# z2's last gelu product and sums by VectorE, its squares by ScalarE; weights split ahead beside the V tiles; distances between loads

## The chip, the cores and the metric

The kernel runs on one core of a Trainium2 chip. The metric is the device time of one execution in microseconds (us), lower is better. A core has TensorE (PE in the profile; its weight loads are PEld), VectorE (DVE), ScalarE (ACT), GpSimd (POOL) and SyncE (SP), which here only issues DMA transfers, in order. Each engine runs its own instructions in the order in which the program lists them, and waits by semaphores for the others.

## The reference

Two branches work on the layer norm of the same x (2048 x 512) and are added to x: attention with 32 heads of 16 columns, and a gated mlp that mixes over the sequence.

```python
def _A_ref(x, wqkv, wo):
    q, k, v = ...                                   # 32 heads, Dh = 16
    scores = jnp.einsum("bhqd,bhkd->bhqk", q, k) * (Dh ** -0.5)
    p = _softmax(scores, axis=-1)
    o = jnp.einsum("bhqk,bhkd->bhqd", p, v)
    return o.transpose(0, 2, 1, 3).reshape(B, S, D) @ wo

def _B_ref(x, w_in, w_sp, b_sp, w_out):             # Fh = 896
    z = _gelu(jnp.einsum("bsd,df->bsf", x, w_in))
    z1 = z[..., :Fh]
    z2 = _layernorm(z[..., Fh:], axis=-1)
    g = jnp.einsum("ts,bsf->btf", w_sp, z2) + b_sp[None, :, None]
    return jnp.einsum("bsf,fd->bsd", z1 * g, w_out)

xn = _layernorm(x, axis=-1)
return x + _A_ref(xn, A_wqkv, A_wo) + _B_ref(xn, B_w_in, B_w_sp, B_b_sp, B_w_out)
```

The gelu is the one with tanh: z (1 + tanh(c (z + 0.044715 z^3))) / 2. The kernel leaves out the half, which the layer norm behind z2 takes out again (so its epsilon is 4 EPS).

## The kernel before

All products with float32 inputs are made of split operands: a high part and the rest (`hi`, `lo`), three products each, so a weight is loaded, copied by POOL (L291) and subtracted by POOL (L293) before TensorE can use it. Weights that are used later than they are split are stored to a DRAM copy and fetched again (`ahead_of_time`, `fetch_parts`: w1 to `w1scr`, the first eight blocks of the spatial weights to `wsscr`).

Attention handles the 32 heads as 16 pairs, each in 64 steps of scores, 1024 steps in all. A step is one score product (L1157), the exponential by ScalarE, and a share of the product with the values (L1258). Ahead of each group of scores runs the row maximum of the next: a product of its own (L1171) whose result VectorE reduces (`mm`, L872); the maxima `ms` go through DRAM (`mscr`) into a row of the queries (`qst`). All this is laid out in 128 **blocks**. A block holds 8 score items, 9 or 7 maxima items in turn, 24 **dense** slots, and at its end a run of 32 matmuls with the values. `ORDER` holds the two patterns, as strings of S, M, D and V.

The dense slots are filled from a queue of generators: `v_rest`, `qk_rest` (queries and keys of the later heads), `z2_all` (16 tiles of 128 rows, 896 columns), `z1_all`, `spatial` (4 groups of 512 rows, 7 units each), `mlp_out`, `attn_out`. Where the queue has nothing ready, the planner writes a **filler** (L1230), two matmuls with a zero weight that add nothing; they keep TensorE busy.

The order of all engines is fixed when the program is built, by a planner. It counts the time of TensorE in `T["P"]` and gives each piece of other work to an engine's clock (`yield "A", us` for ScalarE, `"D"` VectorE, `"G"` POOL) or to a condition (`"C"`); the microseconds there are its own assumptions. Work of low rank on ScalarE and VectorE is placed only in the time of a values run, unless it is older than `AGE` (`may`). The conditions test the planner's time (`clock`) and free buffers (`room`, changed by `lease`): `room["big"]` counts the free buffers of one SBUF ring, from which weights, z tiles and temporaries come. None of this runs on the chip: what runs is the order, with semaphores for data that one engine hands to another and for buffers.

A z2 tile (`z2_norm`, L511) goes from ScalarE (square) to POOL (L518, L520), to ScalarE (tanh), to POOL (L524: 1 + tanh; L526: times z), to VectorE (two `bn_stats` L533, one `bn_aggr` L535), to POOL (six operations of one column, L539 to L544, then the normalised tile as high part and rest, L550 to L554 for 512 and for 384 columns), and by SP to DRAM (`z2scr`), from where the spatial products fetch it as `zs`.

Of the kernel before, what the change touches and what calls it, by code (L numbers as in the profile page):

```python
# [16 lines left out]
P = 128  # L17
# [19 lines left out]
LATE = 24  # L37
LEAD = 30
# [5 lines left out]
AGE = 6.0  # L44
# [16 lines left out]
def fused_block(ctx, tc, x, wqkv, wo, w_in, w_spT, b_sp, w_out, out):  # L61
# [219 lines left out]

    def weight(out, k, a, spare):
        yield "C", lambda: raws[0] < DEEP and room["big"] > 1 + spare[0]
# [23 lines left out]
    def fetch_parts(out, k, scr, spare):  # L307
        yield "C", lambda: room["big"] > 1 + spare[0]
        t = piece(f"wf{len(out)}_{len(wsp)}")
        move(t, scr)  # L310
        yield "T", LOAD
        out[k] = t
# [134 lines left out]
    def qk_rest():  # L447
        for f in range(NF):
            owed[0] += 1
            spawn(ahead_of_time(f, (f"w1_{f}", w_in[:, f * P:(f + 1) * P], D, ND), w1scr[f], AHEAD), 1)  # L450
        for g in (2, 3, 0, 1):
            for m in range(1, 4):
                if m == 2 and g in (3, 0):
                    fetch_xnT((g + 1) % NG, 0.5)
# [4 lines left out]
                if (g, m) in ((3, 1), (0, 1)):  # L459
                    for s in range(KEPT // 2) if g else range(KEPT // 2, KEPT):  # L460
                        owed[0] += 1
                        spawn(ahead_of_time(s, sp_weights(0, s), wsscr[s], AHEAD), 1)
# [26 lines left out]
    def v_rest():  # L489
        for t in range(EARLY, NT, 2):  # L490
# [4 lines left out]
            if t in (2, 6):  # L495
                lease("big", 4)
            yield "e", [v_out(t + b, b) for b in range(2)]
# [13 lines left out]
    def z2_norm(t, z):  # L511
# [5 lines left out]
        yield "G", 1.0  # L517
        nc.gpsimd.tensor_scalar(u, u, 0.044715, 1.0, ALU.mult, ALU.add)  # L518
        yield "G", 2.1
# [3 lines left out]
        yield "G", 1.2  # L523
        nc.gpsimd.tensor_scalar(u, u, 1.0, 1.0, ALU.add, ALU.mult)  # L524
        yield "G", 2.1
        nc.gpsimd.tensor_mul(z, u, z)  # L526
        lease("big", 1)
        st = sm.tile([P, 2, 6], F32, tag="zst", name=f"zst{t}", bufs=6)
        mv = sm.tile([P, 2], F32, tag="zmv", name=f"zmv{t}", bufs=6)
        rs = sm.tile([P, 3], F32, tag="zrs", name=f"zrs{t}", bufs=6)  # L530
        for j in range(2):
            yield "D", 0.62
            nc.vector.bn_stats(st[:, j, :], z[:, j * 448:(j + 1) * 448])  # L533
        yield "D", 0.1
        nc.vector.bn_aggr(mv, st)  # L535
        yield "G", 1.6
        g = nc.gpsimd
        v, r, q, m = rs[:, 0:1], rs[:, 1:2], rs[:, 2:3], mv[:, 0:1]
        g.tensor_scalar(v, mv[:, 1:2], 1.0, 4 * EPS, ALU.mult, ALU.add)  # L539
# [4 lines left out]
        g.tensor_scalar(q, m, r, -1.0, ALU.mult, ALU.mult)  # L544
        for j, (lo, w) in enumerate(((0, 512), (512, 384))):
# [3 lines left out]
            yield "G", 0.0012 * w  # L549
# [828 lines left out]
```

## Time and profile before

| | |
|---|---|
| median of 3 runs | 1856.94 us (1855.68 to 1857.37) |
| profiled execution, its own time | 1855.84 us |
| its span (first to last instruction) | 1853.9 us |
| first values run of attention begins | 114.77 us |
| last values run of 32 matmuls begins | 1805.56 us |
| granted TensorE clock | 0.999 |

The span is what the profile divides into shares. "Busy" is the time in which an engine ran an instruction. The prediction reads three more kinds of rows. In the chain of waits, a row is the start, the length, and what ran or was waited for, followed back from the last instruction of the kernel; `x32` counts matmuls of one line in a row, and `SPq` is a DMA issue on SP's queue. In a group of instructions, `out<-in` names the tiles, then come the shape, the count, the total time, the mean in ns, and the idle time of the engine before them with what ended it. In the timeline, a bracket at the end of a row is the idle time before that instruction and what ended it.

Each group of spatial products uses its own 16 blocks of weights. Around a change of group the blocks 61, 75 and 89 hold 19, 19 and 16 dense slots, and the two or three after each of them up to 27; block 22 in the z2 stage holds none.

### The profile page before, as it was taken

To read this page: it belongs to the slowest core of one execution; us is meant where nothing else is said; L and a number is where in the kernel's file an instruction comes from. 1 tells how busy PE (TensorE), PEld (TensorE's weight loads), DVE (VectorE), ACT (ScalarE), POOL (GpSimd) and SP (SyncE) were. 2 spreads that over 40 slices of the span, in tenths; PEclk is the share of its full clock that TensorE was granted. 3 is DMA by queue.
4 is the path that set the end of the run, shared out by engine and by line. 5 is a ranking of instruction groups with operands and counts; after the bars stand their busy time and mean duration, and the time that the engine had idled before them with its cause. 6 is when DMAs were issued, how large, how long until landed. Compare 5 with 4: busy or idle time off the path is not lost.

```text
span 1853.9 us, 38030 instructions
## 1 busy us (share of the span) xinstructions
PE 1807.5 (97%) x14778; PEld 1093.5 (59%) x14778; DVE 1440.9 (78%) x1677; ACT 1189.6 (64%) x1292; POOL 722.0 (39%) x808
## 2 busy tenths in 40 slices
PE   6999999999999999999999999999999999999998
PEld 4766566655655565556556665666656556565543
DVE  6578778888888787877878787787778878787883
ACT  2157777687776777666666665666656666565665
POOL 5324342778888777222452135102522240002200
PEclk9999999999999999999999999999999999999999
DMA  7728872533565246656867558565767667575422
GB/s 236 288 93 283 277 238 87 127 91 112 133 217 137 100 119 201 152 160 154 219 171 199 156 180 217 155 146 154 194 164 186 177 173 148 149 175 143 130 86 80
DMA packets 212124, 306.14 MB, mean 165 GB/s; under 512 B 36816, under 2 KB 108048, under 8 KB 209056
## 3 DMA queue, kind: packets, MB, share of 16 engines
q1 hardware_dynamic: 202824, 273.83, 53.8%
q0 software_dynamic: 9120, 29.89, 4.7%
q8 instruction: 116, 1.90, 0.4%
q14 instruction: 64, 0.52, 0.1%
HBM read 193.80 MB, written 109.85 MB: 164 GB/s over the span
## 4 chain that ended last, share of the span: by engine, by line
PE 87%; DVE 5%; DMA 2%; ACT 2%; issue 1%; POOL 1%; SPq 1%; DVEq 0%; ACTq 0%; POOLq 0%
PE dps L1216 35%; PE sl L1258 23%; PE sl L1157 14%; PE sl L1171 12%; DVE mm L872 3%; SPq L134 1%; PE dps L1230 1%; ACT pf L78 1%; DMA zs<-z2scr 1%; POOL wsp L293 0%; DMA wsp_11r<-in_w_spT 0%; PE sl L247 0%; PE sl L246 0%; PE sl L245 0%; PE sl L1016 0%
## 5 line engine op out<-in xcount | busy, mean ns | idle before, releaser
L872 DVE TENSOR_REDUCE mm<-sl 128x2 f32<-128x1024 f32 x1024 | 1223.8, 1222 | 202.2 <-PE sl L1171 195.8
L78 ACT ACTIVATE pf<-sl 128x1024 f32<-128x1024 f32 x1024 | 1041.6, 1026 | 335.1 <-PE sl L1157 298.5
L1258 PE MATMUL sl<-pf,vall 128*32 128x512 f32 x4096 | 467.9, 595 | 1.0 <-DVE on L1006 0.6
L1157 PE MATMUL sl<-qst,kst 50*128 50x512 f32 x2048 | 436.0, 418 | 9.4 <-DVE mm L872 2.9
L1171 PE MATMUL sl<-kst,qst 48*128 48x512 f32 x2048 | 422.1, 405 | 4.5 <-DVE mm L872 2.4
L1216 PE MATMUL dps<-wsp,zs 64*128 64x512 f32 x2352 | 379.0, 392 | 1.6 <-DMA zs<-z2scr 1.5
L1157 PEld LDWEIGHTS sl<-qst,kst 50*128 50x128 f32 x2048 | 194.3, 184 | 221.9 <-issue 79.6
L1258 PEld LDWEIGHTS sl<-pf,vall 128*32 128x32 f32 x4096 | 119.3, 109 | 266.9 <-issue 234.3
L1171 PEld LDWEIGHTS sl<-kst,qst 48*128 48x128 f32 x2048 | 195.1, 185 | 105.0 <-ACT pf L78 52.6
L1216 PEld LDWEIGHTS dps<-wsp,zs 64*128 64x128 f32 x2352 | 226.9, 187 | 39.3 <-DMA zs<-z2scr 2.2
L78 ACT ACTIVATE e<-sl 128x512 f32<-128x512 f32 x64 | 38.3, 598 | 205.2 <-PE sl L1258 198.0
L1280 DVE TENSOR_TENSOR e<-sl,e 128x512 f32<-128x512 f32 x64 | 44.3, 692 | 134.3 <-PE sl L1258 76.3
L778 POOL TENSOR_TENSOR hhl<-z1i,hhl 128x512 fp32r<-128x512 f32 x28 | 36.1, 1297 | 267.1 <-ACT hhl L78 267.0
L1216 PE MATMUL dps<-w,xt 64*128 64x448 f32 x768 | 110.4, 368 | 1.5
L1216 PE MATMUL dps<-wout,hp 64*128 64x512 f32 x672 | 110.5, 393 | 0.0
L923 POOL TENSOR_TENSOR ob<-ob 128x512 f32<-128x512 f32 (+1 forms) x16 | 20.6, 1285 | 195.2 <-DMA ob<-rscr 195.2
L1216 PEld LDWEIGHTS dps<-w,xt 64*128 64x128 f32 x768 | 73.5, 186 | 16.3 <-issue 7.8
L1216 PEld LDWEIGHTS dps<-wout,hp 64*128 64x128 f32 x672 | 65.8, 187 | 9.2
L919 POOL TENSOR_TENSOR ob<-ob 128x512 f32<-128x512 f32 (+1 forms) x16 | 20.6, 1287 | 101.6 <-DMA ob<-escr 100.9
L443 POOL TENSOR_TENSOR qkhl<-qr,qkhl 128x512 fp32r<-128x512 f32 x24 | 30.3, 1282 | 70.4 <-ACT qkhl L78 66.3
L1216 PE MATMUL dps<-wf,zs 64*128 64x512 f32 x336 | 55.5, 393 | 0.1
L1216 PE MATMUL dps<-xnT,wqk 64*128 64x512 f32 x288 | 47.7, 396 | 1.1 <-ACT vall L78 0.4
(289 smaller groups left out, 1688.3 us busy)
## 6 DMA issues: line engine op xcount, KB each, us to landing
zs<-z2scr SPq DMA_DIRECT2D x192, 256.0 KB
escr<-e SPq DMA_DIRECT2D x60, 256.0 KB
hscr<-hhl POOLq DMA_DIRECT2D x28, 512.0 KB, 6.4
qst<-qscr SPq DMA_DIRECT2D x30, 384.0 KB
kst<-kscr SPq DMA_DIRECT2D x30, 384.0 KB
qscr<-qkhl SPq DMA_DIRECT2D x16, 512.0 KB
kscr<-qkhl SPq DMA_DIRECT2D x16, 512.0 KB
xscr<-xnT POOLq DMA_DIRECT2D x16, 512.0 KB, 4.8
```

The costliest lines, as they stand in the source:

```text
L78: return nc.scalar.activation(out, in_, func, **kw)
L134: nc.sync.dma_start(raw(dst), raw(src))
L443: nc.gpsimd.tensor_sub(hl[:, 1, :], raw_, hl[:, 0, :].bitcast(F32))
L778: nc.gpsimd.tensor_sub(hl[:, 1, :], z1, hl[:, 0, :].bitcast(F32))
L872: nc.vector.tensor_reduce(mmax[g][:, :, t, kc], sl[k], AX.X, ALU.max)
L919: nc.gpsimd.tensor_add(both_[rows, 0, :], both_[rows, 0, :], both_[rows, 1, :])
L923: nc.gpsimd.tensor_mul(both_[rows, 0, :], both_[rows, 0, :], both_[rows, 1, :])
L1157: nc.tensor.matmul(sl[k][:, j, :], kst[p % 2][rows, kt * P:(kt + 1) * P], qst[p % 2][rows, c * 512:(c + 1) * 512], start=True, stop=True)
L1171: nc.tensor.matmul(sl[k][:, j, :], qst[p % 2][rows, tt * P:(tt + 1) * P], kst[p % 2][rows, kc * 512:(kc + 1) * 512], start=True, stop=True)
L1216: nc.tensor.matmul(dps[:, bank, :w], lhs, rhs, start=go, stop=stop)
L1258: nc.tensor.matmul(sl[k][cols:cols + VW, 0, :], vpack(kt + r, 2 * p + j), pf[:, j * 512:(j + 1) * 512], start=n % CYC == 0, stop=n % CYC = ...
L1280: nc.vector.tensor_add(e, sl[k][:, 0, :], e)
```

## The change

Three things are changed, and the planner's assumed costs with them.

1. **z2.** VectorE forms (tanh + 1) z in two halves of 448 columns, and the same instruction gives the sum of each half. POOL adds the two sums to a negative mean (one column). ScalarE squares z minus the mean over 896 columns, and the same instruction gives the sum of squares. The two wide POOL operations (L524, L526) and the `bn_stats` and `bn_aggr` are gone, and `u` is handed back one step later.
2. **Splitting ahead.** The loads, splits and stores of w1 (seven) and of the first eight spatial weight blocks are asked for behind V tile 6 (`VAHEAD`) in place of inside `qk_rest`.
3. **Distances.** `bulk(us)` notes that the road is taken for so long in the planner's time, `clear()` asks whether it is free: weights keep 1 us, fetched parts and z loads 2 us. A z load that is needed next goes at once. `AGE` goes from 6 to 9, and one fetch of xnT from 0.5 to 1.5.

```diff
--- before.py
+++ after.py
@@ -35,13 +35,14 @@
 DEEP = 4
 ZROOM = 4
 LATE = 24
+VAHEAD = 6
 LEAD = 30
 KEPT = 8
 OUTS = 8
 XAT = 8.0
 XBY = 2.0
 AHEAD = (1,)
-AGE = 6.0
+AGE = 9.0
 GATED = "AD"
 ORDER = ('SMDDSDDMDSDDMDDSDMDDSDMDDSDMDDSDMDDSDDMDMV', 'SMDDDDSDMDDSDMDDSDMDDSDMDDDSDMDDSDDDDMSV')
 PF = 8
@@ -279,8 +280,17 @@
     raws = [0]
     owed = [0]
 
+    road = [0.0]
+
+    def clear():
+        return clock() >= road[0]
+
+    def bulk(us):
+        road[0] = max(road[0], clock()) + us
+
     def weight(out, k, a, spare):
-        yield "C", lambda: raws[0] < DEEP and room["big"] > 1 + spare[0]
+        yield "C", lambda: clear() and raws[0] < DEEP and room["big"] > 1 + spare[0]
+        bulk(1.0)
         raws[0] += 1
         rw = begin(*a)
         n = rw.shape[1]
@@ -305,7 +315,8 @@
         after(2.5, lease, "big", 1)
 
     def fetch_parts(out, k, scr, spare):
-        yield "C", lambda: room["big"] > 1 + spare[0]
+        yield "C", lambda: clear() and room["big"] > 1 + spare[0]
+        bulk(2.0)
         t = piece(f"wf{len(out)}_{len(wsp)}")
         move(t, scr)
         yield "T", LOAD
@@ -445,21 +456,14 @@
         after(2.5, lease, "hilo", 1)
 
     def qk_rest():
-        for f in range(NF):
-            owed[0] += 1
-            spawn(ahead_of_time(f, (f"w1_{f}", w_in[:, f * P:(f + 1) * P], D, ND), w1scr[f], AHEAD), 1)
         for g in (2, 3, 0, 1):
             for m in range(1, 4):
                 if m == 2 and g in (3, 0):
-                    fetch_xnT((g + 1) % NG, 0.5)
+                    fetch_xnT((g + 1) % NG, 1.5)
                 if m == 3 and g == 1:
                     z2_load(0)
                     z2_load(1)
                 yield from need(lambda: (m, 1) in wq)
-                if (g, m) in ((3, 1), (0, 1)):
-                    for s in range(KEPT // 2) if g else range(KEPT // 2, KEPT):
-                        owed[0] += 1
-                        spawn(ahead_of_time(s, sp_weights(0, s), wsscr[s], AHEAD), 1)
                 if g == 1 and m == 1:
                     prepare(w2, [((c, j), f"w2_{c}_{j}", w_in[c * P:(c + 1) * P, FH + j * 448: FH + (j + 1) * 448], 448) for c in range(ND) for j in range(2)], spare=(2,))
                 ops = [lambda c, w=wq[m, a]: (w[:, 0, c * P:(c + 1) * P], w[:, 1, c * P:(c + 1) * P], xnT[g, c][:, 0, :], xnT[g, c][:, 1, :]) for a in range(2)]
@@ -494,6 +498,13 @@
             yield from both(ND, ops(t), ops(t + 1))
             if t in (2, 6):
                 lease("big", 4)
+            if t == VAHEAD:
+                for f in range(NF):
+                    owed[0] += 1
+                    spawn(ahead_of_time(f, (f"w1_{f}", w_in[:, f * P:(f + 1) * P], D, ND), w1scr[f], AHEAD), 1)
+                for s in range(KEPT):
+                    owed[0] += 1
+                    spawn(ahead_of_time(s, sp_weights(0, s), wsscr[s], AHEAD), 1)
             yield "e", [v_out(t + b, b) for b in range(2)]
             yield "q",
 
@@ -514,43 +525,42 @@
         u = piece(f"z2u{t}").bitcast(F32).rearrange("p a b -> p (a b)")[:, :FH]
         yield "A", ta(FH)
         act(u, z, AF.Square)
-        yield "G", 1.0
+        yield "G", 0.98
         nc.gpsimd.tensor_scalar(u, u, 0.044715, 1.0, ALU.mult, ALU.add)
-        yield "G", 2.1
+        yield "G", 2.2
         nc.gpsimd.tensor_mul(u, u, z)
         yield "A", ta(FH)
         act(u, u, AF.Tanh, scale=GC)
-        yield "G", 1.2
-        nc.gpsimd.tensor_scalar(u, u, 1.0, 1.0, ALU.add, ALU.mult)
-        yield "G", 2.1
-        nc.gpsimd.tensor_mul(z, u, z)
+        st = sm.tile([P, 5], F32, tag="zst", name=f"zst{t}", bufs=6)
+        rs = sm.tile([P, 3], F32, tag="zrs", name=f"zrs{t}", bufs=6)
+        g = nc.gpsimd
+        a, b, m, square, v = (st[:, i:i + 1] for i in range(5))
+        for j, half in enumerate((a, b)):
+            cols = slice(j * 448, (j + 1) * 448)
+            yield "D", 0.63
+            nc.vector.scalar_tensor_tensor(z[:, cols], u[:, cols], 1.0, z[:, cols], ALU.add, ALU.mult, accum_out=half)
+        yield "G", 0.6
+        g.tensor_scalar(m, a, b, -1.0 / FH, ALU.add, ALU.mult)
+        yield "A", ta(FH) + 0.2
+        act(u, z, AF.Square, bias=m, accum_out=square)
         lease("big", 1)
-        st = sm.tile([P, 2, 6], F32, tag="zst", name=f"zst{t}", bufs=6)
-        mv = sm.tile([P, 2], F32, tag="zmv", name=f"zmv{t}", bufs=6)
-        rs = sm.tile([P, 3], F32, tag="zrs", name=f"zrs{t}", bufs=6)
-        for j in range(2):
-            yield "D", 0.62
-            nc.vector.bn_stats(st[:, j, :], z[:, j * 448:(j + 1) * 448])
-        yield "D", 0.1
-        nc.vector.bn_aggr(mv, st)
-        yield "G", 1.6
-        g = nc.gpsimd
-        v, r, q, m = rs[:, 0:1], rs[:, 1:2], rs[:, 2:3], mv[:, 0:1]
-        g.tensor_scalar(v, mv[:, 1:2], 1.0, 4 * EPS, ALU.mult, ALU.add)
+        yield "G", 2.2
+        r, q = rs[:, 1:2], rs[:, 2:3]
+        g.tensor_scalar(v, square, 1.0 / FH, 4 * EPS, ALU.mult, ALU.add)
         g.tensor_tensor(r, v, mhalf, ALU.pow)
         g.tensor_scalar(q, r, r, v, ALU.mult, ALU.mult)
         g.tensor_scalar(q, q, -0.5, 1.5, ALU.mult, ALU.add)
         g.tensor_mul(r, r, q)
-        g.tensor_scalar(q, m, r, -1.0, ALU.mult, ALU.mult)
+        g.tensor_mul(q, m, r)
         for j, (lo, w) in enumerate(((0, 512), (512, 384))):
             yield open_("hilo")
             lease("hilo", -1)
             hl = hilo(f"z2hl{t}_{j}")
-            yield "G", 0.0012 * w
+            yield "G", 0.0009 * w + 0.32
             g.tensor_scalar(hl[:, 0, :w], z[:, lo:lo + w], r, q, ALU.mult, ALU.add)
-            yield "G", 0.0012 * w
+            yield "G", 0.0009 * w + 0.32
             g.tensor_scalar(z[:, lo:lo + w], z[:, lo:lo + w], r, q, ALU.mult, ALU.add)
-            yield "G", 0.0025 * w
+            yield "G", 0.0022 * w + 0.24
             nc.gpsimd.tensor_sub(hl[:, 1, :w], z[:, lo:lo + w], hl[:, 0, :w].bitcast(F32))
             for a in range(2):
                 store(z2scr[:, lo // P:(lo + w) // P, a, t, :], hl[:, a, :w].rearrange("p (f q) -> p f q", q=P), 0.3 + 2 * a)
@@ -691,7 +701,8 @@
 
     def z_loader():
         for k in range(len(zparts)):
-            yield "C", lambda: k < zused[0] + 4 and room["big"] > (min(owed[0], ZROOM) if k > zused[0] + 1 and owed[0] else raws[0] > 0)
+            yield "C", lambda: (clear() or k <= zused[0] + 1) and k < zused[0] + 4 and room["big"] > (min(owed[0], ZROOM) if k > zused[0] + 1 and owed[0] else raws[0] > 0)
+            bulk(2.0)
             load_z(k)
 
     def load_z1(g, f):
```

The built program has 178 filler matmuls (206 before); all other matmuls are the same in number. VectorE has 32 `SCALAR_TENSOR_TENSOR` in place of 32 `BN_STATS` and 16 `BN_AGGR`, ScalarE 16 operations of 896 columns more, POOL 32 of 896 columns less.

TensorE at the start of block 22, in the z2 stage, before. `sl` are PSUM banks of scores and maxima, `dps` those of the dense stream, `brow` and `zeror` are the zero operands of a filler:

```order
L1157 MATMUL sl_202<-qst_90,kst_92 128x512 x2
L1171 MATMUL sl_201<-kst_93,qst_91 128x512 x2
L1230 MATMUL dps<-brow,zeror 128x512 x2
L1157 MATMUL sl_203<-qst_90,kst_92 128x512 x2
L1230 MATMUL dps<-brow,zeror 128x512 x2
L1171 MATMUL sl_202<-kst_93,qst_91 128x512 x2
L1230 MATMUL dps<-brow,zeror 128x512 x2
L1157 MATMUL sl_201<-qst_90,kst_92 128x512 x2
L1230 MATMUL dps<-brow,zeror 128x512 x2
L1171 MATMUL sl_203<-kst_93,qst_91 128x512 x2
L1230 MATMUL dps<-brow,zeror 128x512 x2
```

And after the change (`w_0_0` to `w_1_1` are pieces of w2, `xt` the transposed input of a z2 tile):

```order
L1168 MATMUL sl_203<-qst_90,kst_92 128x512 x2
L1182 MATMUL sl_202<-kst_93,qst_91 128x512 x2
L1227 MATMUL dps<-w_0_0_2669,xt_4184 128x448
L1227 MATMUL dps<-w_0_1_2687,xt_4184 128x448
L1227 MATMUL dps<-w_0_0_2669,xt_4184 128x448
L1227 MATMUL dps<-w_0_1_2687,xt_4184 128x448
L1168 MATMUL sl_201<-qst_90,kst_92 128x512 x2
L1227 MATMUL dps<-w_0_0_2669,xt_4184 128x448
L1227 MATMUL dps<-w_0_1_2687,xt_4184 128x448
L1227 MATMUL dps<-w_1_0_2702,xt_4184 128x448
L1227 MATMUL dps<-w_1_1_2719,xt_4184 128x448
```

Before, no dense matmul stands between the scores and maxima of this block, only fillers; after, dense matmuls of a z2 tile stand there.

VectorE around the values run of an odd block of the z2 stage, before. `z_8` and `z_9` are z2 tiles, `zst` and `zmv` their statistics, `mm` the maxima, `e_0` the running sum of the values' product:

```order
L872 TENSOR_REDUCE mm_4929<-sl_201 128x2
L872 TENSOR_REDUCE mm_4929<-sl_203 128x2
L533 BN_STATS zst_4846<-z_8_4353 128x6
L533 BN_STATS zst_5037<-z_9_4621 128x6
L535 BN_AGGR zmv_4847<-zst_4846 128x2
L533 BN_STATS zst_5037<-z_9_4621 128x6
L535 BN_AGGR zmv_5038<-zst_5037 128x2
L1280 TENSOR_TENSOR e_0_4974<-sl_202,e_0_4974 128x512
```

And after (the same place of the next pair of tiles):

```order
L883 TENSOR_REDUCE mm_4968<-sl_201 128x2
L541 SCALAR_TENSOR_TENSOR z_10_4703,zst_5001<-z2u_4819,z_10_4703 128x448
L541 SCALAR_TENSOR_TENSOR z_11_4855,zst_5166<-z2u_4981,z_11_4855 128x448 x2
L1291 TENSOR_TENSOR e_0_5026<-sl_202,e_0_5026 128x512
L883 TENSOR_REDUCE mm_4968<-sl_203 128x2
```

Three `BN_STATS` have become three products with a sum, and the two aggregations are gone; the sum `e_0` stands right behind them in both.

SP's queue in blocks 74 to 76, at a change of the spatial group, before. `zs` are z2 tiles for the spatial products, `wsp_15r` the last weight block of the next group, `ob` and `os` the output of attention:

```order
L134 DMA qst_91<-mscr_165 2x16x32 x2
L134 DMA wsp_15r<-in_w_spT 128x512
L134 DMA qst_90<-qscr_96 48x2048
L134 DMA zs_12671<-z2scr 64x2x512 x2
L134 DMA kst_92<-kscr_100 48x2048
L134 DMA os_3_12575<-escr_3_138 128x1x32 x2
L134 DMA ob_3_12576<-escr_3_138 128x1x512 x2
L134 DMA zs_12703<-z2scr 64x2x512 x2
L134 DMA escr_1_140<-e_1_12569 128x512
L134 DMA zs_12764<-z2scr 64x2x512 x2
```

And after:

```order
L135 DMA escr_0_139<-e_0_12263 128x512
L135 DMA zs_12500<-z2scr 64x2x512 x2
L135 DMA qst_90<-qscr_96 48x2048
L135 DMA zs_12527<-z2scr 64x2x512 x2
L135 DMA kst_92<-kscr_100 48x2048
L135 DMA ob_3_11956<-rscr_3_154 128x1x512
L135 DMA mscr_165<-ms_12553 128x32
L135 DMA qst_90<-qscr_96 48x2048
L135 DMA zs_12582<-z2scr 64x2x512 x2
L135 DMA kst_92<-kscr_100 48x2048
L135 DMA qst_91<-mscr_165 2x16x32 x2
L135 DMA zs_12668<-z2scr 64x2x512 x2
```

Before, one `zs` is asked for between the loads of the next pair of heads (`qst`, `kst`) and one behind those of `os` and `ob`. Now `wsp_15r` is gone ahead, and four `zs` stand ahead of or beside them.

## The prediction

> **What bounds the kernel now.** I read the page first (busy shares, the chain by engine), then the chain of waits in stretches, which gives the start of each values run and so the length of every attention block, then the engines' busy time in one pair of blocks of each stage, and last the groups of instructions that the change touches.
>
> ```profile
> PE 1807.5 (97%) x14778; PEld 1093.5 (59%) x14778; DVE 1440.9 (78%) x1677; ACT 1189.6 (64%) x1292; POOL 722.0 (39%) x808
> PE 87%; DVE 5%; DMA 2%; ACT 2%; issue 1%; POOL 1%; SPq 1%; DVEq 0%; ACTq 0%; POOLq 0%
> 432.69:461.15 28.46, 27.75 (x234) 17.27 (x238) 22.96 (x28) 21.00 (x24) 22.62 (x24) 1.00 0.42 122
> 710.16:737.33 27.17, 27.08 (x231) 16.83 (x234) 21.76 (x25) 20.18 (x24) 21.87 (x24) 1.00 0.71 224
> 843.90:870.58 26.68, 26.68 (x232) 16.20 (x234) 21.78 (x27) 17.84 (x19) 5.51 (x5) 1.00 0.67 173
> ```
>
> The three lower rows are stretches of two blocks in the z2, the z1 and the spatial stage: start and end, length, then busy time (and instructions) of PE, PEld, DVE, ACT, POOL, the granted clock, the DMA share and GB/s. PE is full in all three: 26.68 of 26.68 us in the spatial stage. So two blocks with everything on time take 26.7 to 28.5 us, and TensorE sets that. In the z2 stage VectorE (22.96), ScalarE (21.00) and GpSimd (22.62) leave 5.5 to 7.5 us of each pair free. An engine's work can therefore save time in two ways only: PE items that do no useful work disappear, or a PE wait does. PE's idle time is 1853.9 − 1807.5 = 46.4 us in all.
>
> The useless items are the fillers (L1230), which the planner writes where it believes that no dense matmul is ready:
>
> ```profile
> L1230 PE MATMUL dps<-brow,zeror 64*128 64x512 f32 x206 | 39.3, 408 | 0.5 <-ACT z1x L78 0.3
> 755.56 0.46 PE dps L1230 x4
> ```
>
> Four of them in a row hold PE for 0.46 us, so an item (two matmuls on two halves of the array) costs 0.23 us, and all 103 cost at most 24 us. The waits sit where blocks come out longer than their neighbours. A row of the chain has the start, the length and what ran; these are the values runs that I use and three waits beside them:
>
> ```profile
> 129.58 3.57 PE sl L1258 x32
> 145.11 3.57 PE sl L1258 x32
> 182.75 1.21 SPq L134
> 184.01 5.82 DMA qst<-mscr
> 200.44 3.60 PE sl L1258 x32
> 254.51 3.57 PE sl L1258 x32
> ...
> 294.57 3.57 PE sl L1258 x32
> 406.32 3.57 PE sl L1258 x32
> 419.71 3.57 PE sl L1258 x32
> 432.69 3.57 PE sl L1258 x32
> 531.15 3.57 PE sl L1258 x32
> 545.31 3.69 PE sl L1258 x32
> 560.45 3.57 PE sl L1258 x32
> ...
> 1085.73 3.57 PE sl L1258 x32
> ...
> 1141.65 10.77 DMA zs<-z2scr
> 1156.24 3.57 PE sl L1258 x32
> 1169.89 3.57 PE sl L1258 x32
> 1317.27 3.57 PE sl L1258 x32
> 1373.91 3.57 PE sl L1258 x32
> 1508.33 3.57 PE sl L1258 x32
> ```
>
> Numbering the values runs from 0 at 114.8 us, block 22 (406.32 to 419.71) took 13.39 us though it held no dense matmul at all, where two blocks with 48 of them take 28.46 (first of the lower rows above): starving a block gives almost nothing back, since its maxima keep VectorE busy. The work left out then comes later in a block of its own. The chain also shows what late data cost: the tile zs, issued at 1141.65, was 10.77 us on its way, and the values run behind it began at 1156.24.
>
> **The change, part by part.** The sum is made against the profiled run: 1855.84 us, span 1853.9, so 1.94 us lie around the span. It stands 1.1 us below the median of 1856.94.
>
> *POOL and DVE work of a z2 tile.*
>
> ```profile
> L526 POOL TENSOR_TENSOR z<-z2u,z 128x896 f32<-128x896 f32 x16 | 33.8, 2110 | 0.3
> L524 POOL TENSOR_SCALAR z2u<-z2u 128x896 f32<-128x896 f32 x16 | 15.0, 940 | 31.7 <-ACT z2u L78 31.5
> L533 DVE BATCH_NORM_STATS2 zst<-z 128x6 f32<-128x448 f32 x32 | 18.9, 611 | 3.1 <-POOL z L526 3.1
> L535 DVE BATCH_NORM_AGGREGATE zmv<-zst 128x2 f32<-128x12 f32 x16 | 3.2, 204 | 0.3
> L78 ACT ACTIVATE z2u<-z 128x896 f32<-128x896 f32 x16 | 15.1, 946 | 0.8 <-DVE z L506 0.8
> ```
>
> The nearest rows of VectorE with two SBUF inputs are two lines of their own (count, then the shortest, median and longest in ns), and three rows of the timeline:
>
> ```profile
> L268 DVE TENSOR_TENSOR wqk<-wqk_0r,wqk x1: 681/681/681, 15.3 to 15.3; 128x512 fp32r<-128x512 f32 x1
> L915 DVE TENSOR_TENSOR os<-os x16: 176/181/1032, 818.0 to 1761.8; 128x32 f32<-128x32 f32 x12, 96x32 f32<-96x32 f32 x4
> 464.84 0.69 DVE L1280 TENSOR_TENSOR e<-sl,e 128x512 f32<-128x512 f32 x1 [1.21 <-PE sl L1258]
> 898.86 1.27 POOL L778 TENSOR_TENSOR hhl<-z1i,hhl 128x512 fp32r<-128x512 f32 x1 [22.03 <-ACT hhl L78]
> 899.15 1.03 DVE L915 TENSOR_TENSOR os<-os 128x32 f32<-128x32 f32 x1
> ```
>
> Per tile POOL loses 2.110 + 0.940 = 3.05 us, with two tiny operations more; ScalarE gains one square of 0.946; VectorE loses 2 x 0.611 + 0.204 = 1.43 and gains two half products with a sum. Of these the trace has none. The nearest row is L268, a VectorE operation with the same two SBUF f32 inputs, 512 wide in 0.681: scaled to 448, 0.60, so 1.20 against 1.43, a gain of 0.2. The upper bound is POOL's own product of the same tensors, 2.110 for 896, so 1.055 for 448, and the wait behind POOL: the operation of L915 is 0.18 us alone, and 1.03 when it began inside POOL's L778 and ended with it, 0.85 more. I take 0.61, because L268 is the same engine with the same kinds of operands, and L915 had company in 3 of 16 cases only.
>
> That is the one place where a page speaks against the change. In the Trainium skill, "SBUF — State Buffer", section "SBUF: two separate sides", a VectorE operation with two SBUF inputs and a GpSimd operation take one exclusive port pair for a whole instruction; the trace agrees (0.18 against 1.03). "Vector Engine (DVE) Microarchitecture Reference", section "Points that are easy to get wrong", has it that this form with two f32 SBUF sources runs at half throughput, as an estimate some 0.47 us more per half product; L268, another form with such operands, doesn't show it. By that page the 32 products would add 15 us of VectorE work, and by both a product could take 0.61 + 0.47 + 0.85 = 1.93, which is the case of rival 2.
>
> Where does it stand? In the z2 stage the half products are queued on VectorE with the maxima of the scores, one or three of them beside a values run. There VectorE stood idle 1.21 us before the running sum of L1280, which holds a PSUM bank that the next scores need. With 0.61 each the new queue (3 x 0.61 = 1.83) is shorter than the old one (3 x 0.61 + 2 x 0.204 = 2.24), so nothing is late. POOL's 3.05 us lay in free time and buy nothing by themselves. What they buy is the order: a tile's chain is shorter, the planner finds the next tile's room sooner, and block 22 is no longer starved. The order shows, for a z2 pair, 1 filler in place of 3, so 28.46 − 2 x 0.23 = 28.0. Before, the z2 stage is the 19 blocks from 294.57 to 560.45, 265.88 us. After, the same dense slots fit 18 blocks: eight pairs of 28.0 and one starved pair of about 27 (blocks 22 and 23 took 26.37, a full pair 28.46), together 251; the block saved here reappears at the end with fewer dense slots, half of a spatial or attention pair, 13.5. 251 + 13.5 is 264.5: **−1**, from −8 (shorter chain, no waits at 545 and 560) to +18 (worked out with the slow rival below).
>
> *Splitting w1 and the first half of the spatial weights ahead, from blocks 1 to 7 to V tile 6.*
>
> ```profile
> 95.00:115.00 20.00, 18.43 (x150) 13.34 (x150) 16.61 (x20) 11.45 (x13) 0.00 (x0) 1.00 0.00 1
> 145.00:160.00 15.00, 14.91 (x128) 8.62 (x130) 11.15 (x11) 10.50 (x13) 5.62 (x5) 1.00 1.00 306
> ```
>
> From 95 to 115 us POOL and the DMA engines were empty, from 145 to 160 the DMA engines were full at 306 GB/s. Fifteen loads of 0.26 MB, fifteen stores of 0.52 MB and fifteen splits move from the second stretch into the first. Those 11.8 MB take 39 us at 306 GB/s, so a part still lies beside blocks 0 and 1, where the stores stand ahead of the first maxima loads on SP. Two places were late. Four good blocks took 254.51 − 200.44 = 54.07, so 13.5 each. Block 2 took 145.11 − 129.58 = 15.53, with one dense slot more (0.23): 1.8 lost. Blocks 3 to 6 took 55.33, and in the last of them PE waited for the maxima's load of 5.82 us: 1.3 lost. If that traffic is gone, 3.1 come back. Half a microsecond to one may be lost ahead (a guess between none and the 1.3 of that load), as two splits of the first scores' data wait behind the new ones. I take **−2**, from −3.5 to +2.
>
> *Loads at a distance of each other (clear, bulk), AGE 9, and the planner's new costs.* These add no instruction and no wait that runs; they change the place of loads in SP's queue and of tasks on ScalarE and VectorE. In the spatial stage the weights of the next group are now asked for one by one earlier, and the zs tiles get ahead: the zs that block 76 waited for was asked for in blocks 75 and 76 and now is in block 74. The six blocks from 1085.73 to 1169.89 took 84.16 us where three good pairs take 80.04: 4.1 lost. Blocks 89 to 92, from 1317.27 to 1373.91, took 56.64 where two pairs take 53.36: 3.3 lost. After the change these blocks have 24 dense slots each, no starving and no catching up. The starved pairs 45/46 and 60/61 stay. So **−7**, from 0 (other loads come late in their place) to −11: that is the whole excess of the spatial stage, 1508.33 − 737.33 = 771.0 for 57 blocks less 28.5 x 26.68 = 760.4.
>
> *Fillers later on.* In the mlp_out stage an even block had one filler and now has none: 8 less, 8 x 0.23 = 1.8, of which I take **−1.5** because one or two of them covered a wait of 0.14 us per odd block. In the last blocks 18 dense items move ahead and fillers stand in their place, in all four items less, **−1**, from −2 to 0.
>
> Sum: −2 − 1 − 7 − 1.5 − 1 = −12.5, so a span of 1841.4 and a run of 1843.3; against the median of the runs 1844.4. I say 1844.
>
> **Rivals.**
>
> 1. *Only the fillers go.* If the long blocks around 1156 and 1374 are bound by something that the order does not touch (a block of 19 dense slots is followed by two of 27 and 26, and such work is only moved), what is left is 206 − 178 = 28 matmuls, 14 items of 0.23: −3.2, so 1852.6. For it: block 22 shows that a block without dense work is hardly shorter. Against it: the chain names the DMA of zs there, and 19 + 27 + 26 slots are the work of three full blocks of 24.
>
> 2. *The half products are slow, and the kernel gets slower.* If each takes 1.055 and waits 0.85 behind POOL, three of them take 5.7 beside a values run in place of 2.24, which is 3.5 more; 1.21 is free, so the sum of L1280 and with it a PSUM bank are 2.3 late in each of 8 odd blocks, 18 us, and the −1 of that stage is lost: 1855.84 − 12.5 + 1 + 18 = 1862.3. It decides from about 1.7 us for a product and its wait: 3 x 1.7 − 2.24 − 1.21 = 1.65, times 8 is 13. For it: L915. Against it: after the change POOL has nothing of the same tile to do while they run; only the neighbour tile's operations can be in the way.
>
> 3. *The early stores push the first blocks.* The stores of w1 stand ahead of the first maxima load on SP. A transfer was 5.82 us late once; if the first two of them are, and the rest goes as forecast, 1850 to 1856.
>
> 4. *Loads at a distance come late.* A spacing of 2 us for tiles of which one is used in some 4 us (192 tiles in 771 us) leaves half the pace; if each of the four group changes then waits 3 us, as at 1156, the −7 turns into +5: 1855.
>
> **How the numbers follow.** The forecast has 0.64, rival 1 0.12, rival 2 0.14, rivals 3 and 4 0.10 together. Runs of this kernel differ by 0.1%; I call it the same within 0.2%, 3.7 us, so 1853.2 to 1860.6. Faster: 0.64 + two thirds of rival 1 (0.08) + 0.03 of the last = 0.75. Same: 0.04 + 0.06 + 0.01 from rival 2 = 0.11. Slower: the rest of rival 2 and 0.01 = 0.14. The forecast's own range is 1835 to 1850. For 8 in 10 the range goes from 1834 to 1858: it holds rival 1 and most of 3 and 4, and leaves out rival 2 and the best ends of all terms together.
>
> **What would show it.** Right: fillers down to 178; the new VectorE group near 0.61 us; z2 pairs of 28.0; blocks 72 to 77 and 89 to 92 at 80.0 and 53.4; blocks 2 and 6 at 13.8. Wrong: the new group above 1 us with L1280 waiting for VectorE instead of PE; waits on zs at other group changes; a longer stretch up to the first values run at 114.77.

## The result and the profile after

The changed kernel takes 1849.42 us (median of 7 runs, 1846.96 to 1853.61), the kernel before 1856.6 (7 runs, 1854.06 to 1858.39). The ratio is 0.9964, 95% interval [0.9954, 0.9974]: it is faster by 0.36%, about 7 us. The forecast was 1844. The profiled execution of the changed kernel took 1850.6 us, its span 1848.7; against the span of before that is −5.2 us, and the sums below are made against this one. It is one of three among the seven runs with a mean granted clock of 0.995 (1850.22 to 1853.61 us); the four others, with 0.997 or 0.998, took 1846.96 to 1849.42.

The page of the changed kernel, busy time by engine and the chain by engine:

```profile
PE 1807.0 (98%) x14750; PEld 1093.0 (59%) x14750; DVE 1440.0 (78%) x1693; ACT 1210.0 (65%) x1324; POOL 683.7 (37%) x792
PE 92%; DVE 5%; issue 1%; ACT 1%; DMA 1%; POOL 1%; DVEq 0%; ACTq 0%; POOLq 0%
```

Then the two-block stretches of the z2, z1 and spatial stages (same columns as in the prediction), and the chain's values runs at the places that the prediction used:

```profile
451.96:479.84 27.88, 26.87 (x231) 17.11 (x234) 23.54 (x33) 23.17 (x28) 20.58 (x30) 1.00 0.39 115
711.00:738.20 27.20, 26.83 (x222) 15.39 (x226) 21.58 (x24) 19.81 (x23) 21.78 (x24) 1.00 0.60 168
844.73:871.55 26.82, 26.68 (x231) 16.45 (x234) 20.64 (x25) 16.79 (x17) 3.90 (x4) 1.00 0.43 122
```

```profile
120.28 3.57 PE sl L1269 x32
135.07 3.58 PE sl L1269 x32
150.51 3.57 PE sl L1269 x32
...
204.61 3.59 PE sl L1269 x32
...
298.79 3.57 PE sl L1269 x32
...
574.80 3.57 PE sl L1269 x32
...
1087.98 3.57 PE sl L1269 x32
1101.63 3.57 PE sl L1269 x32
1114.79 3.60 PE sl L1269 x32
...
1169.88 3.57 PE sl L1269 x32
...
1317.85 3.57 PE sl L1269 x32
...
1371.63 3.59 PE sl L1269 x32
...
1506.22 3.57 PE sl L1269 x32
```

PE is as busy as before in sum (1807.0 against 1807.5), but the chain has 5% more of PE in it and no SP queue. The z2 pair is 27.88 (28.46 before), the pair of the spatial stage 26.82, so 0.14 *more* than before (26.68). And the first values run begins at 120.28 in place of 114.77: 5.5 us are lost before the first block ends. From the start of block 14 to the end of block 33 it was 279.75 and is 276.01 (574.80 − 298.79). The six blocks up to 1169.88 took 81.90 (84.16 before), the four up to 1371.63 took 53.78 (56.64 before).

Summed by stage, from the starts of the values runs of the two profiled executions:

| stretch | before | after | difference | forecast |
|---|---|---|---|---|
| up to the first values run | 114.7 | 120.2 | **+5.5** | with the next row |
| blocks 1 to 13 (qk) | 179.8 | 178.5 | −1.3 | −2 |
| blocks 14 to 33 (z2) | 279.8 | 276.0 | −3.7 | −1 |
| blocks 34 to 44 (z1) | 149.8 | 149.9 | +0.1 | 0 |
| blocks 45 to 102 (spatial) | 784.2 | 781.5 | −2.7 | −7 |
| blocks 103 to 116 (mlp_out) | 188.4 | 186.3 | −2.0 | −1.5 |
| blocks 117 to the end | 157.3 | 156.2 | −1.1 | −1 |

The new VectorE operations and the new square, from the groups of instructions (shape, count, total us, mean ns, idle time before):

```profile
L541 DVE SCALAR_TENSOR_TENSOR z<-z2u,z 128x448 f32<-128x448 f32 x32 | 19.1, 618 | 4.8 <-ACT z2u L79 4.8
L541 DVE DVE_READ_ACCUMULATOR z<-z2u,z 128x1 f32 x32 | 2.6, 82 | 0.0
L79 ACT ACTIVATE z2u<-z,zst 128x896 f32<-128x896 f32 x16 | 16.8, 1047 | 0.1
L529 POOL TENSOR_SCALAR z2u<-z2u 128x896 f32<-128x896 f32 x16 | 16.3, 1022 | 39.8 <-ACT z2u L79 39.2
```

A half product takes 0.618 and the read of its sum 0.082; none took over 0.626, so none was held up by a POOL operation. The new square takes 1.047, and the read of its sum another 0.203. Of POOL's operations on a z2 tile only L529 became longer, 1.022 on average where it was 0.941; no run shows why.

### The profile page after: what moved, and what is told of

It reads as the page before. It is cut to its first block, busy times and chain, and to the rows that moved or that the text cites. A ratio compares the mean times of both kernels' runs of the same rounds, so it can differ in the third digit from the quotient of the medians.

```text
span 1848.7 us, 38046 instructions
## 1 busy us (share of the span) xinstructions
PE 1807.0 (98%) x14750; PEld 1093.0 (59%) x14750; DVE 1440.0 (78%) x1693; ACT 1210.0 (65%) x1324; POOL 683.7 (37%) x792
## 4 chain that ended last, share of the span: by engine, by line
PE 92%; DVE 5%; issue 1%; ACT 1%; DMA 1%; POOL 1%; DVEq 0%; ACTq 0%; POOLq 0%
PE dps L1227 36%; PE sl L1269 25%; PE sl L1168 14%; PE sl L1182 13%; DVE mm L883 4%; PE dps L1241 1%; ACT pf L79 0%; PE sl L248 0%; PE sl L247 0%; PE sl L1027 0%; PE sl L246 0%; DVE bst L352 0%; DMA mscr<-ms 0%; ACT vall L79 0%; DMA x<-in_x 0%
## 5 line engine op out<-in xcount | busy, mean ns | idle before, releaser
L1227 PE MATMUL dps<-wsp,zs 64*128 64x512 f32 x2352 | 383.4, 392 | 0.1
```

What stands on the lines that cost most here:

```text
L1227: nc.tensor.matmul(dps[:, bank, :w], lhs, rhs, start=go, stop=stop)
```

## The experiments

**Where do the 5.5 us ahead of the first values run come from?** The chain of waits of the changed kernel, in the gap:

```profile
98.68 4.55 DMA mscr<-ms
103.23 0.02 issue
103.25 2.23 DMA qst<-mscr
105.48 0.14 issue
105.62 0.94 PE sl L1168 x2
...
108.15 0.43 PE sl L1168 x2
```

The timeline of VectorE (first row) and of SP's queue (the others), start and duration of the issue:

```profile
91.98 0.21 DVE L900 STREAM_TRANSPOSE ms<-mrow 128x32 f32<-128x32 f32 x1
...
94.49 1.58 SPq L135 DMA_DIRECT2D w1scr<-w  x2
96.13 0.59 SPq L135 DMA_DIRECT2D w_3r<-in_w_in  x1
97.65 0.40 SPq L135 DMA_DIRECT2D w1scr<-w  x1
98.14 0.44 SPq L135 DMA_DIRECT2D w_4r<-in_w_in  x1
98.68 1.16 SPq L135 DMA_DIRECT2D mscr<-ms  x1
```

The first maxima `ms` are ready at 92.2. Their store to `mscr` stands on SP's queue behind three stores of split weights, and those wait for POOL's splits (the last of the three is issued at 97.65, when POOL has finished that weight). So the store of the maxima is issued at 98.68. It needs 4.55 us while the DMA engines are full (a share of 1.05 from 98 to 102), and TensorE, which needs the maxima back in `qst` for its first scores, waits 2.2 us, until 105.62. In the kernel before, nothing stood ahead of that store:

```profile
91.72 0.34 SPq L134 DMA_DIRECT2D mscr<-ms  x1
```

In the changed kernel a matmul pair then takes 0.43 us in place of 0.23. The granted clock by stretches of 2 us (the columns as above):

```profile
104.00:106.00 2.00, 0.38 (x1) 0.18 (x1) 0.00 (x0) 0.00 (x0) 1.92 (x3) 1.00 0.23 88
106.00:108.00 2.00, 2.00 (x16) 1.57 (x17) 0.24 (x1) 1.03 (x1) 1.00 (x1) 0.90 1.04 379
108.00:110.00 2.00, 2.00 (x11) 1.45 (x10) 1.09 (x2) 1.39 (x2) 0.00 (x0) 0.50 1.00 295
110.00:112.00 2.00, 2.00 (x10) 1.33 (x10) 2.00 (x2) 1.55 (x3) 0.26 (x1) 0.50 1.00 354
```

*Split back in its old place.* Everything else of the change stays, and so does TensorE's order:

```diff
 def qk_rest():
+    for f in range(NF):
+        owed[0] += 1
+        spawn(ahead_of_time(f, (f"w1_{f}", ...), w1scr[f], AHEAD), 1)
...
+            if (g, m) in ((3, 1), (0, 1)):
+                ... # sp_weights as before
 def v_rest():
-        if t == VAHEAD: ...
```

> The changed kernel, with the splitting of w1 and of the spatial weights put back where it was before the change (inside qk_rest); TensorE's order is the same as in the changed kernel. Theory 1 (the early loads and stores stand ahead of the first maxima on SP's queue, TensorE waits some 2.4 us at 103 us and then runs at half clock for 6 us): the first values run begins at 114.8 us instead of 120.2, block 6 takes 15.0 again instead of 13.8, the run is 4 to 4.5 us below the changed kernel, about 1845. Rival (the low clock at 108 us is chance and the move itself is worth the 1.2 us of block 6): no earlier than the changed kernel, 1849 to 1851, and low clock near 108 us in some runs of this kernel too.

Measured: 1845.77, ratio to before 0.9941 [0.9928, 0.9954]. The first values run begins at 114.2. Block 6 was 13.8 here too, not 15.0 (block 10 has a wait of its own, 14.8 in place of 13.8), so in the changed kernel the gain at block 6 does not need the move.

*The move alone, in the kernel before* (`VAHEAD = 6`, and the requests taken out of `qk_rest`):

> The kernel before with the split ahead at V tile 6 alone; TensorE's order is that of before. Theory 1: first values run at about 120, block 6 at 13.8 instead of 15.0, so 4 us above the kernel before, about 1860. Rival (the head of the changed kernel was chance): 1855.5, 1.2 below it.

Measured: 1860.87, ratio 1.0024 [1.0014, 1.0035]: 4 us slower than before. Block 6 took 13.8 here. Its first values run begins at 120.16 behind the same two DMA rows (5.03 and 2.19 us), and the clock is 0.71 from 105 to 111 us. Of the six kernels profiled up to there (the two compared, these two, and `VAHEAD = 12` and the stage begun later, below), the three with this wait had a low clock behind it, the three without had none.

*TensorE kept busy in the wait:*

```diff
 k = take("s")
+for n in range(20 if n_st == 0 else 0):
+    j = n % 2
+    nc.tensor.matmul(sl[k][:, j, :], zeror[64 * j:64 * j + 64], brow[64 * j:64 * j + 64], start=True, stop=True)
 for j in range(2):
```

> The changed kernel with ten more filler items (zero products into the PSUM bank that the first scores then overwrite) ahead of the first score product, so that TensorE is busy for 2.3 us of its wait for the first maxima; all else is the same. Theory 1a (the wait of over 2 us is what lowers TensorE's clock): no stretch at half clock between 105 and 117 us, the first values run begins at 117 to 118 instead of 120.2, the run is 2 to 3 us below the changed kernel, about 1847. Rival (the clock falls there for another reason, such as the full DMA engines): low clock stays, first values run at 120 or later, 1849 to 1851.

Measured: 1848.33, ratio 0.9952 [0.9937, 0.9966]; the first values run begins at 117.9, 2.3 us earlier. Its stretch at the same place, at full clock beside DMA engines as full as ever:

```profile
108.00:111.00 3.00, 2.35 (x18) 1.33 (x16) 3.00 (x3) 2.89 (x4) 1.03 (x2) 1.00 0.98 350
```

So of the 5.5 us about 3.2 are the wait and 2.3 the half clock that comes behind it. In the times of whole runs the second part is not resolved (1848.33 against 1849.42).

*The split a little later:* `VAHEAD = 12`, nothing else.

> The changed kernel with VAHEAD 12 instead of 6: the first maxima go through SP's queue ahead of all new loads and stores. Theory 1: first values run at 114.8, block 6 still 13.8, so 5.5 us below the changed kernel, about 1844. Rival (the same traffic then meets the second and third maxima, in blocks 1 to 3): one of the blocks 1 to 4 takes 1 to 3 us longer, 1845.5 to 1848.

Measured: 1844.01 (6 runs, 1842.26 to 1847.02), ratio 0.9933 [0.9919, 0.9947]. First values run at 113.22, block 6 at 13.8, no new wait in blocks 1 to 4. It beats both kernels.

**Why did the spatial stage gain 2.7 and not 7?** In the changed kernel an odd block of the stage takes 13.16 in the median (12.97 before) and an even one 13.66 (13.71). The rows above show it: 1101.63 − 1087.98 = 13.65 and 1114.79 − 1101.63 = 13.16. A unit of the stage fills two blocks. Before, units began in even blocks, now in odd ones. In the trace of the changed kernel an odd block now holds either the item for the bias (blocks 49 and 53) or a TensorE wait of 0.14 in front of its first scores (blocks 47 and 51); before, blocks 49, 51 and 53 hold neither. The next kernel is the changed one with the stage begun one block later, all distances kept:

```diff
 def spatial():
+    yield "w", 22.0
     for n, (g, (x, y)) in enumerate(units):
```

> The changed kernel with the start of the spatial stage held back by 22 us of the planner's time, so that its units begin in even blocks, as before the change; all distances between loads stay. Theory 2 (what the spatial stage gained and lost hangs on whether units begin in odd or even blocks): odd blocks take 12.96 instead of 13.16 (28 x 0.2 = 5.6 less), the starved blocks 61, 75, 89 and their catch-up blocks come back (4 to 6 more), the mlp stage costs 0.28 more in each of 7 pairs (2 more), the tail 0.5 more: 1850 to 1853. Rival, the reason given in the prediction (the distances between loads keep the group changes free of waits): the group changes stay as in the changed kernel, 1845 to 1847.

Measured: 1856.15, ratio 0.9996 [0.9984, 1.0007]: all of the gain is gone, more than expected. In its chain of waits an odd block is 1031.90 − 1018.93 = 12.97 and an even one 13.69, and the late zs at the group change is back:

```profile
1018.93 3.57 PE sl L1270 x32
1031.90 3.57 PE sl L1270 x32
1045.59 3.57 PE sl L1270 x32
...
1140.82 11.20 DMA zs<-z2scr
1157.37 3.57 PE sl L1270 x32
```

Against the changed kernel blocks 72 to 77 take 3.6 more and 89 to 92 take 2.8 more, the other 48 blocks of the stage 3.2 less, the mlp stage 1.8 more, the end 1.0 more. With the distances in place the starved blocks 61, 75 and 89 and the wait for zs return. So the distances alone do not keep the group changes clean; all kernels measured with clean ones have units that begin in odd blocks. A part of the loss is the clock: block 76 took 18.41 (16.70 in the kernel before), and behind its wait for zs, from 1153.2 to 1156.6, the granted clock was 0.5.

*The same shift in the kernel before* (the same line, nothing else):

> The kernel before with the start of the spatial stage held back by 22 us of the planner's time and nothing else: its units begin in odd blocks, without any distances between loads. Theory 2: odd spatial blocks 13.16 instead of 12.96, blocks 89 to 92 without starving near 53.7 instead of 56.6, mlp pairs 26.6 instead of 26.9; a starved pair at 45 and 46 and a later end of the dense stream cost some back: 1852 to 1856. Rival (only the distances keep the group changes free): blocks 89 to 92 stay above 55.5 and the run comes to 1857 to 1861.

Measured: 1858.21, ratio 1.0012 [1.0002, 1.0022], in time inside the rival's range. Blocks 89 to 92 took 54.7 (56.6 before, 53.7 expected by theory 2), odd blocks 13.17, the mlp stage 1.1 less: in these parts theory 2 is nearer. But the wait for zs moved to block 75 (16.4), the six blocks to 77 took 0.8 more than before, and the other 48 blocks of the stage 4.5 more, since their odd ones are longer. Shifting the units is thus not enough for the gain; without distances one late zs stays.

**What moved the units, and what did each part of the change do alone?** Two kernels with one part each. The new `z2_norm` with its planner costs, in the kernel before (`AGE` stays 6):

> The kernel before with the new z2_norm and its planner costs alone. Theory 3 (the z2 part pays only together with the distances, which let the planner use the shorter chain): its order has blocks 20 and 21 starved in place of 22 and as many blocks to the end of the z2 stage, so the z2 stage is within 1 us of before, and the run is 1855 to 1857. Rival (POOL's 3 us less per tile pay by themselves): z2 stage 3 to 4 us shorter, 1852 to 1853.

Measured: 1864.65, ratio 1.0044 [1.0029, 1.0058]: 8 to 9 us slower, outside both expectations. The distances (`clear`, `bulk`, 1.5 for xnT) with `AGE` 9, in the kernel before:

> The kernel before with the distances between loads and AGE 9 alone (clear, bulk, fetch_xnT 1.5). Its order has the spatial units begin in odd blocks. Theory 2 (odd or even): odd spatial blocks 13.16, blocks 89 to 92 near 53.7 and 75 to 77 near 41, mlp pairs 26.6, z2 stage as before; one more starved pair in the z1 stage: 1851 to 1854. Rival, the prediction's term of -7 for the distances by themselves: 1847 to 1849.

Measured: 1863.83, ratio 1.004 [1.0026, 1.0055]: also 8 us slower, and outside both. Its z2 stage took 284.1 (279.8 before) and the spatial stage 784.0, as long as before: the units begin in odd blocks and no block from 89 to 92 is starved, but these four took 56.2, because TensorE waited in block 92 for maxima whose store took 11.3 us. So the place of the units and the distances together are not enough either. Each part alone loses, and together (the kernel with the split in its old place) they gain 10.4. One place in the profile of the kernel with the new `z2_norm` alone, its chain of waits, then the timeline:

```profile
321.51 1.05 issue
322.56 0.63 DVE z L506
323.19 0.02 issue
323.21 0.55 ACT z L78
323.76 0.04 issue
323.81 0.96 PE dps L1229 x4
324.76 3.60 PE sl L1257 x32
```

```profile
320.12 2.53 DVE L871 TENSOR_REDUCE mm<-sl 128x2 f32<-128x1024 f32 x2 [0.38 <-PE sl L1170]
321.62 0.94 ACT L78 ACTIVATE z2u<-z2u 128x896 f32<-128x896 f32 x1
322.56 0.61 DVE L506 COPY z<-dps 128x448 f32<-128x448 f32 x1
```

The fillers (L1229) come late here: they write a PSUM tile that ScalarE copies out first (`z L78`), ScalarE's copy waits for VectorE's copy of the other half (`z L506`), and that one stands behind two maxima. The tanh of a tile stands at 321.62, ahead of the values run instead of within it; that it held up anything in this place is not shown. What the two traces do show is the order. In this kernel 20 of the 48 operations of ScalarE on z2 tiles begin outside a values run, in the changed kernel 10; and the blocks 14 to 33 hold 122 filler matmuls against 44. Whether such work may stand outside a values run is what `AGE` says: 6 us in the kernel before, 9 in the changed one. In the changed kernel the tanh stands at 328.20, inside the values run.

So `AGE` was taken apart from the distances. *The changed kernel with AGE 6:*

```diff
-AGE = 9.0
+AGE = 6.0
```

> The changed kernel with AGE 6 instead of 9, one digit. Theory 4 (AGE decides whether the new z2 chain pays: with 6 its operations on ScalarE and VectorE are placed outside the values runs): the z2 stage is near 286 us as with the new z2_norm alone, units begin in even blocks and blocks 61, 75 and 89 starve; with the late first maxima this gives 1866 to 1870. Rival (AGE is a detail, the new z2 chain and the distances carry the gain): 1848 to 1852.

Measured: 1873.16, ratio 1.0084 [1.0068, 1.0101], above both expectations. One digit turns 7 us of gain into 16 of loss. The z2 stage took 287.0, as theory 4 has it, again with 20 of the 48 operations outside the values runs. The spatial stage took 789.2, where block 76 alone, with its wait for zs, took 20.6.

*The new z2_norm and AGE 9 in the kernel before, no distances, no move:*

> The kernel before with the new z2_norm, its planner costs and AGE 9, without distances and without the split ahead. Theory 4: the z2 stage is near 276 us as in the changed kernel; without the distances the group changes starve two pairs (60 and 61, 75 and 76) and the dense stream ends one block later; block 6 at 15.0: 1848 to 1853. Rival (the z2 stage needs the distances too): z2 stage at 280 or above, 1856 or more.

Measured: 1849.65, ratio 0.9954 [0.994, 0.9969]. The z2 stage lies between these two rows of its chain; the second fence has the same two of the kernel with the new `z2_norm` and AGE 6:

```profile
292.41 3.57 PE sl L1257 x32
...
568.64 3.57 PE sl L1257 x32
```

```profile
295.58 3.57 PE sl L1257 x32
...
582.00 3.64 PE sl L1257 x32
```

They are the values runs of the blocks 13 and 33: 276.2 us lie between them with AGE 9, 286.4 with AGE 6; of ScalarE's 48 operations on z2 tiles 10 begin outside the values runs in place of 20, and there are 48 filler matmuls in place of 122. In the spatial stage its units begin in odd blocks (13.15 in the median), but without distances block 92 waits for late maxima here too (15.6), and the blocks 89 to 92 take 55.9.

*AGE 9 alone in the kernel before:*

> The kernel before with AGE 9 alone. Its order has the dense stream end three blocks later, with 54 dense items behind the last full block. Theory 4 (AGE 9 fits the new z2 chain only, the old one gets later with it): z2 stage 280 or above, more starved blocks, 1861 to 1868. Rival (AGE 9 is better by itself): below 1855.

Measured: 1866.59, ratio 1.0048 [1.0031, 1.0065]. The four corners of the z2 stage (blocks 14 to 33, us):

| | old z2_norm | new z2_norm |
|---|---|---|
| AGE 6 | 279.8 (before) | 286.4 |
| AGE 9 | 284.3 | 276.2 |

Whole runs go the same way: +9 us for either edit alone against the runs of before beside it, −8 for both. Of the +9 of AGE 9 alone only 4.6 lie in the z2 stage, though; 9.6 lie behind block 116, where its order ends the dense stream later, and the spatial stage gained 3.2. The distances on top of both (the kernel with the split in its old place) bring the ratio from 0.9954 to 0.9941, with intervals that overlap.

*A last variant,* VAHEAD 12 with AGE 8:

> The changed kernel with VAHEAD 12 and AGE 8: the same starved blocks as with VAHEAD 12 and AGE 9, and two filler items fewer, 0.5 us. Expected 1843 to 1844.5, that is no difference from VAHEAD 12 alone that these runs can tell.

Measured: 1845.56, ratio 0.9931 [0.9915, 0.9948]: no difference from VAHEAD 12 with AGE 9.

## Why the prediction was right or wrong

The sign and the range were right. The sum was −12.5, the profiled executions differ by −5.2 and the medians by −7.2, so three of its steps were off. Errors of both signs are in it: the z2 stage gained 2.7 more than forecast, the move and the distances together 10.5 less. That the total came out inside the range is in part luck.

- **The half products.** Taken at 0.61 from L268, measured 0.618, and 0.082 for the read of the sum, which the prediction did not have. By the Trainium skill, "VectorE: DVE Perf Modes", section "Two Vector instructions with no wait between them", an operation that also writes out its accumulator is two instructions; the trace agrees. The trace of before also had a row of the same form, which the prediction did not use: L756, `SCALAR_TENSOR_TENSOR` of 512 columns with one source in PSUM, 0.685 in the mean, as fast as L268. ScalarE's square was taken at 0.946 and is 1.25 with the read of its sum. Rival 2 is refuted: the longest of 32 took 0.626. The rule of half throughput for this form with two f32 sources (the Trainium skill, "Vector Engine (DVE) Microarchitecture Reference", section "Points that are easy to get wrong") does not hold here: 448 columns in 0.618, a `bn_stats` of 448 with one source in 0.611.
- **The z2 stage: −1, measured −3.7.** The pair was forecast at 28.0 and is 27.88. The term was too small mainly because it left out the waits in blocks 31 and 32, which it put into its lower bound alone: these blocks took 29.30 before and 27.12 after. The mechanism was only half right. "A tile's chain is shorter, the planner finds the next tile's room sooner" fails by itself: alone the new chain costs 7 us in this stage. It needs AGE 9.
- **The move of the splits: −2, measured +4.2** (head and qk together). The step that failed is "half a microsecond to one may be lost ahead": the sum saw that the stores stand ahead of the first maxima on SP and named it as rival 3, but priced it in the sum with at most the 1.3 of one late load. What it missed is that the stores wait for POOL in an in-order queue (6.5 us for the maxima), and that TensorE's clock falls behind a wait of 2.2 us. The prediction's own sign of being wrong, a longer stretch up to the first values run, came true. Block 6 came down by 1.2 as forecast, but does so without the move too; block 2 stayed (15.43 after, 15.53 before). The DMA engines were not full there: their share over block 2 was 0.51 before and 0.69 after, so the 1.8 us put down to that traffic have another cause, which no run shows.
- **The distances: −7, measured −2.7 for the stage.** The group changes gained 2.3 and 2.9, 5.1 of the 7.4 forecast there, but 2.4 of that went to the other blocks, of which the odd ones are each 0.2 longer; the sum did not have this. And the cause was misnamed: with all distances in place and the units begun in even blocks, the group changes are as bad as before. The prediction read in the order that those blocks are full, and put it down to the loads; it filed AGE under the edits that only "change the place of loads in SP's queue and of tasks on ScalarE and VectorE".
- **mlp_out −1.5, measured −2.0; the end −1, measured −1.1.** Right in size, but for the mlp stage not block by block. The stage has no fillers left, and a pair of blocks is 0.27 shorter, near the price of one. But the even blocks, which held the fillers, fell only from 13.73 to 13.67, and the odd ones, which held none, from 13.17 to 12.96: a TensorE wait of 0.14 in front of their first scores is gone. And in the spatial stage of the changed kernel even blocks with a filler and without are equally long (13.67 and 13.66), so 0.23 for each filler is not a price that holds everywhere. The stage hangs on the block in which units begin as well: with the stage begun later it has its fillers, its waits of 0.14 and its 188.1 again. The end has a disturbance in it: in the profiled execution the last 7 us ran at a granted clock of 0.5, with TensorE 3.9 us busy in place of 3.0.

What stays open: why some orders keep the group changes clean and others, with the units in the same blocks, have late maxima there; what took the wait out of block 6 in kernels without the move (13.8 with the new `z2_norm` and AGE 9, 15.2 with AGE 6); by which waits AGE 6 lengthens the z2 stage, beyond the fillers that its order holds; and how much of the last 2 to 4 us between the new `z2_norm` with AGE 9 and the kernel with all but the move is due to the distances.

## What to carry to other kernels

Before work is moved into an idle stretch, look at what stands in the in-order queue that it passes: a store that waits for a slow engine holds back everything behind it, however small and urgent. Where a planner writes the order, an edit is priced together with the planner's thresholds: two edits that each lost 9 us gained 8 together, so the order is compared edit by edit. And where work repeats with the period of two slots, the slot in which it begins is a cost of its own, here 0.14 us for each pair of blocks in one stage, with the sign turned in the next.

## What the runs showed of the hardware

In all four kernels where TensorE waited over 2 us for the first maxima (2.06 to 3.37 us), the granted clock then fell to 0.5, for 3.4 or 6.8 us; ten useless items in the wait prevented it. Shorter waits had it at times: of the 22 waits between 0.9 and 1.9 us that the fourteen traces hold behind the first 40 us, seven had such a stretch within 3 us behind them. In the kernel with the distances alone the clock was 0.83 and 0.85 over 10 us around waits of 1.53 and 1.24 us (at 244.7 and 556.6), while 1.65 us at 1356 in the kernel with the new `z2_norm` and AGE 9 left it alone. The Trainium skill, "TensorE: Matmul & The Clock Gate", section "What's actually happening", has the array go to half rate after an idle window of about 3.4 us, and the window run freely. The half rate, the lengths of 3.4 and 6.8 us and the dependence on more than the length of a wait agree; that the array must stand idle for 3.4 us does not, as all these waits were shorter.
